# A linear-attention block with a gate: mean and scale of eleven row tiles spread through DRAM, and the order of the steps around it

## The chip, the cores and the metric

The kernel runs on one core of one Trainium2 chip. The metric is the device time of one execution in microseconds.

## The reference

For x of 2048 rows and 576 columns (one batch), with 32 heads of 18 columns:

```python
xn = layernorm(x)                       # (x - m) / sqrt(v + 1e-5)
q, k, v = split(xn @ wqkv)              # 32 heads of 18
phi = lambda t: where(t > 0, t + 1, exp(t)) + 1e-6
pq, pk = phi(q), phi(k)
kv  = einsum("bhsd,bhse->bhde", pk, v)  # one 18 x 18 state per head
z   = einsum("bhsd->bhd", pk)
o   = einsum("bhqd,bhde->bhqe", pq, kv) / (einsum("bhqd,bhd->bhq", pq, z) + 1e-6)
s   = o @ wo
g   = silu((gelu(x @ w_gate) * (x @ w_up)) @ w_down)   # 4608 inner columns
out = x + s * g
```

The change concerns the layer normalization and the order in which k, v, the state `kv` and some of the q products are made.

## The kernel before

**Rows and words.** The 2048 rows are 16 tiles of 128, four tiles to a block (`TT` = 4), and two blocks to each half `s`; `N0` = 8 is the first tile of the second half. The 576 columns are two halves of 288, each laid out as 128 + 128 + 32, the 32 columns three times over. A float32 operand of a long product is cut into two words: a high word, copied by ScalarE (ACT) to the type fp32r, and a low word, the difference, taken by VectorE (DVE). `to_operand` (L281) makes both words of a tile of x: one ACT copy of 384 columns and two DVE subtractions for each of its halves. A product of two such operands takes seven passes for a half, so a part of a tile is 14 matmuls. The weights of k and v are cut into three parts of 416, 412 and 388 columns (`TW`), so a tile has 42 matmuls.

**Normalization.** Tiles 0 to 3 are normalized by rows and then turned by TensorE (PE). Tiles 4 to 15 are loaded twice, two tiles at a time (`load_x`): by rows for the moments, and already turned. `spread` (L169) takes mean and variance with bn_stats and starts the scale with ACT's logarithm and exponential; `scales` (L185) refines the scale on DVE by one step of Newton; `x_next(n)` is both of them for tiles n and n+1. That leaves a mean and a scale on each row's partition, while the turned tile has the rows along its columns and needs both values on all partitions. For this `turn` (L208) lets PE turn the mean and the scale of each row, each taken 128 times over, into a PSUM tile `ms`:

```python
pin(nc.tensor.transpose(t[:, i * P : (i + 1) * P], v.to_broadcast([P, P]), ident))  # L214
```

`normalize` (L228) then is one DVE subtraction of 768 columns and two DVE products of 384, with `ms` as second operand, and `to_operand` behind it. `place(n)` calls it for tiles 4 to 15, `save` does nothing for these.

**A tile of k and v.** `kv_tile(t)` (L492) writes out this order, and `pin` keeps it on every engine: part 0 of the tile's products (`x_mm`); on even t the products of the pair t-2, t-1 that add to the state (`kv_pair`, `kv_mm`; 20 short matmuls for each tile, into the PSUM tile `kv_a`, column groups 0 to 3 of 126 and group 4 of 72); `turn(t+1)`; `k_post(t, 0)`, which evacuates k's columns of part 0 (DVE, `e_k` and `pk`); part 1; `place(t+1)`; `k_post(t, 1)`, at whose end ACT takes the exponential of `e_k` and GpSimd (POOL) adds it to `pk`; `v_post(t, 1)`, ACT's copies of v to `va`; part 2; the steps in `end`, with the moments of later tiles among them; and `v_post(t, 2)`. A tile t with t mod 8 = 7 does not prepare its follower.

**Buffers.** The products of k, v and q, and `ms`, share six PSUM banks; `kv_a` has its own. `pk`, `va` and three pieces of a sum share four SBUF slots. `gl_tile` hands out six SBUF slots that the q tiles use too.

**Between tiles 7 and 8, and behind tile 15.** Four q products for each of two blocks come between tiles 7 and 8 (`q_store`: 14 matmuls, an evacuation in `phi` with ACT, DVE and a POOL add, and a store to DRAM), and for the other two behind tile 15 (`q_hold`, kept in SBUF). The dictionaries `behind` and `ahead` place other steps behind each: moments, sums of x for the fast products of the gate (`difference`; `form` and `form_apart` make words of a sum and store them), the masked state (`kv_done`) and its product with wo (`kv_wo`). The fifth group of a q block (`gi` = 4) is only four transposes. `prep_q`, in tiles 4 to 7, cuts the weights of q, with the subtractions on POOL.

**Queues.** Loads and stores are issued by SyncE (SP) in program order. `load_x(n+4)` stands behind tiles 4, 6, 8 and 10, `form("T4")` with its store at the end of tile 9.

Of the kernel before, what the change touches and what calls it, by code (L numbers as in the profile page):

```python
# [8 lines left out]
F32 = mybir.dt.float32  # L9
# [82 lines left out]
def block_kernel(ctx, tc, x, xe, xt, wq_d, wkv_d, wo, wgu_d, wd_d, out):  # L92
# [92 lines left out]
    def scales(n0):  # L185

        n, mv, st = mom.pop(n0)
        v, r, c = (st[:, i, 0:n] for i in range(1, 4))
        if n == 1:
            vec("tensor_scalar", c, r, r, -0.5, op0=ALU.mult, op1=ALU.mult)  # L190
            vec("tensor_scalar", c, c, v, 1.5, op0=ALU.mult, op1=ALU.add)
            vec("tensor_scalar", c, c, r, None, op0=ALU.mult)
        else:
            vec("scalar_tensor_tensor", c, r, -0.5, r, op0=ALU.mult, op1=ALU.mult)
            vec("tensor_mul", c, c, v)
            vec("scalar_tensor_tensor", c, c, 1.5, r, op0=ALU.add, op1=ALU.mult)
        for t in range(n):
            scale_of[n0 + t] = mv[:, t, 0:1], c[:, t : t + 1]

    def center(n):  # L200

# [6 lines left out]
    def turn(n, new=bank):  # L208

        xs = xstat[n // 2][:, n % 2]  # L210
        if n >= TT:
            xts[n] = t = bank(f"ms_{n}")
            for i, v in enumerate(scale_of.pop(n)):
                pin(nc.tensor.transpose(  # L214
                    t[:, i * P : (i + 1) * P], v.to_broadcast([P, P]), ident
                ))
            return
        tiles = [new(f"xt_{n}_{j}") for j in range(2)]
        xts[n] = [t[:, 0 : 3 * P].rearrange("p (k t) -> p k t", k=3) for t in tiles]
        for j in range(2):  # L220
            for k in range(3):
                pin(nc.tensor.transpose(xts[n][j][:, k, :], xs[:, j, k * P : (k + 1) * P], ident))
# [4 lines left out]

    def normalize(n, s, b, c):  # L228

        ms = xts.pop(n)  # L230
        xs = xstat[n // 2][:, n % 2, D:].rearrange("p (k t) -> p k t", k=6)
        m, r = (ms[:, None, i * P : (i + 1) * P] for i in range(2))
        vec("tensor_sub", xs, xs, m.to_broadcast([P, 6, P]))
        for j, nm in enumerate(BS[b]):
            if nm not in xo[s]:
                xo[s][nm] = big(2 * b + j, [P, 5, TBN], F32R, f"xo_{s}_{nm}")
                new_plain(s, nm)
            vec(
                "tensor_mul", xf[s][nm][:, :, c], xs[:, 3 * j : 3 * j + 3],
                r.to_broadcast([P, 3, P]),  # L240
            )
        for nm in BS[b]:
            to_operand(xo[s][nm], xf[s][nm], c)
# [32 lines left out]
        if last:  # L276
            xts.pop(n)

    mom, scale_of, xts = {}, {}, {}

    def to_operand(o, src, c):  # L281
        act(o[:, 0:3, c], src[:, :, c], AF.Copy)
# [110 lines left out]
        act(e, e, AF.Exp, scale=-1.0)  # L393
        pool("tensor_add", o, o, e)

    def kv_mm(t):
        if t == 0:
            acc.append(own_bank("kv_a"))
        pk, va = pks.pop(t), vas.pop(t)
        for gi, wdt in enumerate(WIDTHS):  # L400
            for half in range(2):
                o, cs = kv_out(gi, half)
                mm(
                    o, va[:, 2 * gi + half, 0 : o.shape[0]],
                    pk[:, gi * GW + cs.start : gi * GW + cs.stop],
                    start=(t == 0 and gi == 0), stop=(t == S // P - 1),
                    skip_group_check=True,
                )
# [8 lines left out]
    def x_mm(t, c, js=(0, 1), passes=KV_PASSES):  # L417

        tb, i = divmod(t, TT)
        s, b = divmod(tb, 2)  # L420
        begin = (t, c) not in pkv
        if begin:
            pkv[t, c] = bank(f"kv_{t}_{c}")
        o = pkv[t, c]
        for j in js:
            for n, (wi, xi) in enumerate(passes):
                mm(
                    o[:, 0 : TW[c]], xo[s][BS[b][j]][:, xi, i * P : (i + 1) * P], kv_part(c, j, wi),
                    start=(begin and j == 0 and n == 0), stop=(j == 1 and (wi, xi) == (2, 2)),
                )  # L430
# [61 lines left out]
    def kv_tile(t, mid_=(), end=()):  # L492

        ahead = t % (2 * TT) != 2 * TT - 1
        x_mm(t, 0)
        if t % 2 == 0:
            kv_pair(t)
        if ahead:
            turn(t + 1)
        k_post(t, 0)  # L500
        x_mm(t, 1)
        if ahead:
            place(t + 1)
            save(t + 1)
        run(list(mid_))
        k_post(t, 1)
        v_post(t, 1)
        x_mm(t, 2)
        run(list(end))
        v_post(t, 2)  # L510

    def kv_pair(t):

        for i in (t - 2, t - 1):
            if i in vas:
                kv_mm(i)

    ph, ph_d = {}, {}

# [904 lines left out]
    def x_next(n):  # L1424

        if n % 2 == 0:
            spread(n, 2)
            scales(n)
        center(n)
# [17 lines left out]
    load_q(0)  # L1447
    for n in range(3, 2 * TT):
        ends = []
        if n < 2 * TT - 2:  # L1450
            ends.append(lambda n=n: x_next(n + 2))
        if n >= TT:
            j, c = divmod(n - TT, 2)
            prep_q(c, j)
            if n == TT + 1:
                load_q(1)
        if n == 2 * TT - 1:
            ends += [lambda i=i: difference(0, i) for i in range(3)]
        kv_tile(n, end=ends)
        if n in (4, 6):  # L1460
            load_x(n + 4, 2)
        if n == TT:
            for nm in BS[0]:
                keep(0, nm, xo[0][nm])
        if n == TT:
            q_store(0, 4)
        if n == TT + 3:
            keep(0, "B22", xo[0]["B22"])
# [3 lines left out]
    def form(nm):  # L1472
        keep(0, nm, build(0, nm, 12))

    def form_apart(nm):
# [11 lines left out]
        dma(out=d[:, 2], in_=last[:, 0].bitcast(F32))  # L1487

    behind = {
        (0, 0): [lambda: kv_pair(N0), lambda: spread(N0, 2), lambda: difference(0, 3)],  # L1490
        (0, 1): [
            lambda: scales(N0), lambda: form("T1"), lambda: q_store(1, 4),
        ],
        (0, 2): [lambda: form_apart("T3")],
        (0, 3): [lambda: turn(N0)],
        (1, 0): [lambda: place(N0)],
        (1, 1): [lambda: form("T2"), lambda: spread(N0 + 2, 2), lambda: scales(N0 + 2)],
    }
# [3 lines left out]
            run(behind.get((tb, gi), []))  # L1502
    for n in range(N0, 2 * N0):
        ends = []
        if n < 2 * N0 - 2:
            ends.append(lambda n=n: center(n + 2) if n == N0 else x_next(n + 2))
        if n == N0 + 1:
            ends.append(lambda: form("T4"))
        if n == 2 * N0 - 3:
            ends.append(load_wo)  # L1510
        if n == 2 * N0 - 2:
            ends.append(make_sel)
        if n == 2 * N0 - 1:
            ends += [lambda i=i: difference(1, i) for i in range(3)]
        kv_tile(n, end=ends)
        if n in (N0, N0 + 2):
            load_x(n + 4, 2)
    ahead = {
        (2, 0): [lambda: kv_pair(2 * N0), kv_done, spread_sel, lambda: difference(1, 3)],
        (2, 1): [lambda: kv_wo(4), lambda: q_hold(2, 7, 4)],  # L1520
        (2, 2): [lambda: kv_wo(0), lambda: kv_wo(1), move_rows],
        (2, 3): [lambda: kv_wo(2), lambda: kv_wo(3)],
        (3, 0): [lambda: den(2), lambda: q_hold(3, 8, 4)],
# [117 lines left out]
```

## Time and profile before

| | |
|---|---|
| median of three runs | 1456.73 us (1456.26 to 1457.28) |
| profiled execution | 1456.62 us |
| its span in the trace | 1454.9 us |
| granted TensorE clock | 1.0 |
| busy: PE, weight loads | 1447.7 us (100%), 1290.2 us (89%) |
| busy: DVE, ACT, POOL | 1152.8 us (79%), 562.5 us (39%), 579.1 us (40%) |
| DMA | 233.98 MB, 161 GB/s in the mean |

Times of instructions are us in one profiled execution; a line number L126 is that of the helper that records every DVE operation (L123 is ACT's, L129 PE's matmuls, L132 POOL's), so a group is told by its tiles, written out<-in. PEld is the loading of PE's weights, which overlaps its matmuls, and SPq the queue of DMA issues. In the chain of waits a line gives the start in us, the step's length, engine, tile, line and the count of instructions. In the view by groups, three figures after a count are the shortest, the median and the longest in ns, followed by when the first and the last began. A releaser row ("PEld ms <- DVE st") gives the summed idle time, the number of waits and the longest, in us.

### The profile page before, as it was taken

To read this page: it belongs to the slowest core of one execution; us is meant where nothing else is said; L and a number is where in the kernel's file an instruction comes from. 1 tells how busy PE (TensorE), PEld (TensorE's weight loads), DVE (VectorE), ACT (ScalarE), POOL (GpSimd) and SP (SyncE) were. 2 spreads that over 40 slices of the span, in tenths; PEclk is the share of its full clock that TensorE was granted. 3 is DMA by queue.
4 is the path that set the end of the run, shared out by engine and by line. 5 is a ranking of instruction groups with operands and counts; after the bars stand their busy time and mean duration, and the time that the engine had idled before them with its cause. 6 is when DMAs were issued, how large, how long until landed. Compare 5 with 4: busy or idle time off the path is not lost.

```text
span 1454.9 us, 22180 instructions
## 1 busy us (share of the span) xinstructions
PE 1447.7 (100%) x8286; PEld 1290.2 (89%) x8286; DVE 1152.8 (79%) x1605; ACT 562.5 (39%) x914; POOL 579.1 (40%) x520
## 2 busy tenths in 40 slices
PE   9999999999999999999999999999999999999998
PEld 8989989988888888888888888888889999999998
DVE  7687767376787887887778878787888978989898
ACT  6443355332222233322322232332235555545454
POOL 3342340225756567565575765667632000000000
PEclk9999999999999999999999999999999999999999
DMA  5543115521432315224242243324389888767886
GB/s 222 191 191 140 38 31 211 211 107 51 161 102 107 130 51 186 90 94 138 77 155 87 100 147 108 110 88 132 115 282 343 263 263 254 246 189 233 278 288 222
DMA packets 118085, 233.98 MB, mean 161 GB/s; under 512 B 11018, under 2 KB 44682, under 8 KB 116058
## 3 DMA queue, kind: packets, MB, share of 16 engines
q1 hardware_dynamic: 115178, 220.31, 44.8%
q0 software_dynamic: 2656, 12.06, 2.2%
q8 instruction: 65, 1.06, 0.3%
q14 instruction: 42, 0.34, 0.1%
q10 hardware_dynamic: 144, 0.20, 0.0%
HBM read 149.91 MB, written 82.58 MB: 160 GB/s over the span
## 4 chain that ended last, share of the span: by engine, by line
PE 94%; DVE 3%; DMA 2%; issue 0%; ACT 0%; SPq 0%; POOL 0%; DVEq 0%; ACTq 0%; POOLq 0%
PE bd L129 21%; PE al L859 16%; PE de L859 16%; PE ga L859 16%; PE kv L129 8%; PE be L859 8%; PE s L129 4%; PE q L129 4%; DMA raw_h<-hs 1%; DVE sx L126 1%; PE kv_a L129 1%; DMA sx<-in_x_dram 0%; DVE raw_h L126 0%; DVE acc L126 0%; PE idle L129 0%
## 5 line engine op out<-in xcount | busy, mean ns | idle before, releaser
L132 POOL TENSOR_TENSOR sm<-raw 128x384 f32<-128x384 f32 x72 | 75.5, 1048 | 146.7 <-DMA raw<-in_wgu_dram 104.8
L129 PE MATMUL kv<-wkv,xo_B 128*128 128x412 f32 (+2 forms) x662 | 125.5, 348 | 0.0
L126 DVE TENSOR_TENSOR wa<-sm,wa 128x768 fp32r<-128x768 f32 x72 | 95.1, 1321 | 36.1 <-ACT wa L123 35.3
L129 PEld LDWEIGHTS kv<-wkv,xo_B 128*128 128x128 f32 x662 | 119.9, 188 | 1.0 <-ACT xo_B L123 0.2
L129 PE MATMUL bd<-w_head,hi 128*128 128x288 f32 x516 | 117.9, 294 | 0.0
L126 DVE TENSOR_TENSOR wa<-raw,wa 128x256 fp32r<-128x256 f32 x72 | 67.7, 940 | 51.5 <-ACT wa L123 48.3
L126 DVE TENSOR_TENSOR wb<-raw,wb 128x256 fp32r<-128x256 f32 (+1 forms) x108 | 101.9, 944 | 7.3 <-ACT wb L123 5.8
L123 ACT ACTIVATE hi<-raw_h 128x1024 fp32r<-128x1024 f32 x59 | 62.6, 1061 | 95.5 <-PE bd L129 65.3
L129 PE MATMUL bd<-w_end,hi 128*128 128x288 f32 x448 | 89.8, 294 | 0.0
L123 ACT ACTIVATE spot_h<-spot_h 128x512 f32<-128x512 f32 x49 | 30.8, 635 | 150.1 <-DVE spot_h L126 150.1
L126 DVE TENSOR_TENSOR raw_h<-raw_h,hi 128x1024 fp32r<-128x1024 f32 x59 | 71.8, 1223 | 20.3 <-ACT hi L123 20.2
L129 PEld LDWEIGHTS bd<-w_head,hi 128*128 128x128 f32 x516 | 87.0, 188 | 0.1
L129 PE MATMUL bd<-w_end,raw_h 128*128 128x288 f32 x264 | 77.9, 295 | 0.0
L123 ACT ACTIVATE wa<-sm 128x1152 fp32r<-128x1152 f32 x36 | 41.8, 1162 | 87.8 <-PE de L859 87.8
L123 ACT ACTIVATE u<-al 128x512 f32<-128x512 f32 x72 | 41.0, 594 | 89.5 <-PE al L859 81.2
L129 PEld LDWEIGHTS bd<-w_end,hi 128*128 128x128 f32 x448 | 71.9, 188 | 0.0
L129 PE MATMUL bd<-beside,raw_h 128*128 128x288 f32 x240 | 70.8, 295 | 0.0
L132 POOL TENSOR_TENSOR spot_h<-spot_h,spot_h 128x512 f32<-128x512 f32 x45 | 62.5, 1396 | 2.9 <-DVE spot_h L126 2.4
L859 PE MATMUL al<-xo_B,wa 128*128 128x512 f32 x252 | 63.0, 389 | 0.0
L859 PE MATMUL al<-xr_B,wa 128*128 128x512 f32 x252 | 63.0, 389 | 0.0
L859 PE MATMUL be<-xo_T,wa 128*128 128x512 f32 x252 | 63.0, 389 | 0.0
L859 PE MATMUL be<-xr_T,wa 128*128 128x512 f32 x252 | 63.0, 389 | 0.0
(274 smaller groups left out, 4040.6 us busy)
## 6 DMA issues: line engine op xcount, KB each, us to landing
raw_h<-hs SPq DMA_DIRECT2D x176, 256.0 KB
raw<-in_wgu_dram SPq DMA_DIRECT2D x36, 768.0 KB
hs<-spot_h SPq DMA_DIRECT2D x90, 256.0 KB
hs<-spot_g SPq DMA_DIRECT2D x80, 256.0 KB
b<-in_wd_dram SPq DMA_DIRECT2D x42, 432.0 KB
hs<-spot_m SPq DMA_DIRECT2D x38, 256.0 KB
raw_g<-hs SPq DMA_DIRECT2D x22, 256.0 KB
raw_a<-hs SPq DMA_DIRECT2D x20, 256.0 KB
```

The costliest lines, as they stand in the source:

```text
L123: pin(nc.scalar.activation(*args, **kw))
L126: pin(getattr(nc.vector, op)(*args, **kw))
L129: pin(nc.tensor.matmul(*args, **kw))
L132: pin(getattr(nc.gpsimd, op)(*args, **kw))
L859: nc.tensor.matmul(o, w[0:rows, wi, :], xop[0:rows, xi, :], start=(start and n == 0), stop=(n == len(PASSES) - 1), skip_group_check=True,)
```

## The change

`scales` for tiles 4 and on copies the two means beside the two scales, writes these 128 x 4 values to DRAM (`md`), and reads them back into all partitions (`mr`, 128 x 4 values on each, in a `gl_tile` slot). `normalize` takes mean and scale of tiles 5 to 15 from there, with steps of four values; `turn` remains for tile 4 alone. In `kv_tile`, for tiles from 5 on that prepare a follower, `place(t+1)` goes ahead of `k_post(t, 0)`. `kv_pair` does groups 0 to 3 of both tiles and then group 4 of both. The moments of tiles 6 and 7 move from the end of tile 4 to that of tile 3, those of 12 and 13 from tile 10 to 9, those of 14 and 15 from tile 12 to 11; `form("T4")` moves from the end of tile 9 to that of 10. Two transposed q groups move one place forward, `q_store(1, 4)` behind the first q product and `q_hold(2, 7, 4)` behind the first of block 2; `turn(8)` goes.

```diff
--- before.py
+++ after.py
@@ -196,6 +196,17 @@
             vec("scalar_tensor_tensor", c, c, 1.5, r, op0=ALU.add, op1=ALU.mult)
         for t in range(n):
             scale_of[n0 + t] = mv[:, t, 0:1], c[:, t : t + 1]
+        if n0 >= TT:
+            vec("tensor_copy", st[:, 3, 2:4], mv[:, 0:2, 0])
+            d = dr.tile([P, 4], F32, name=f"md_{n0}")
+            g = gl_tile([P, P, 4], f"mr_{n0}")
+            dma(out=d, in_=st[:, 3, :])
+            dma(
+                out=g.rearrange("p t c -> p (t c)"),
+                in_=d.rearrange("t c -> (t c)")[None, :].to_broadcast([P, 4 * P]),
+            )
+            for t in range(n):
+                rows_of[n0 + t] = [g[:, None, :, i + t] for i in (2, 0)]
 
     def center(n):
 
@@ -208,7 +219,9 @@
     def turn(n, new=bank):
 
         xs = xstat[n // 2][:, n % 2]
-        if n >= TT:
+        if n > TT:
+            return
+        if n == TT:
             xts[n] = t = bank(f"ms_{n}")
             for i, v in enumerate(scale_of.pop(n)):
                 pin(nc.tensor.transpose(
@@ -227,9 +240,12 @@
 
     def normalize(n, s, b, c):
 
-        ms = xts.pop(n)
+        if n in xts:
+            ms = xts.pop(n)
+            m, r = (ms[:, None, i * P : (i + 1) * P] for i in range(2))
+        else:
+            m, r = rows_of.pop(n)
         xs = xstat[n // 2][:, n % 2, D:].rearrange("p (k t) -> p k t", k=6)
-        m, r = (ms[:, None, i * P : (i + 1) * P] for i in range(2))
         vec("tensor_sub", xs, xs, m.to_broadcast([P, 6, P]))
         for j, nm in enumerate(BS[b]):
             if nm not in xo[s]:
@@ -276,7 +292,7 @@
         if last:
             xts.pop(n)
 
-    mom, scale_of, xts = {}, {}, {}
+    mom, scale_of, xts, rows_of = {}, {}, {}, {}
 
     def to_operand(o, src, c):
         act(o[:, 0:3, c], src[:, :, c], AF.Copy)
@@ -393,11 +409,11 @@
         act(e, e, AF.Exp, scale=-1.0)
         pool("tensor_add", o, o, e)
 
-    def kv_mm(t):
-        if t == 0:
+    def kv_mm(t, groups):
+        if not acc:
             acc.append(own_bank("kv_a"))
-        pk, va = pks.pop(t), vas.pop(t)
-        for gi, wdt in enumerate(WIDTHS):
+        pk, va = pks[t], vas[t]
+        for gi in groups:
             for half in range(2):
                 o, cs = kv_out(gi, half)
                 mm(
@@ -492,14 +508,17 @@
     def kv_tile(t, mid_=(), end=()):
 
         ahead = t % (2 * TT) != 2 * TT - 1
+        early = ahead and t > TT
         x_mm(t, 0)
         if t % 2 == 0:
             kv_pair(t)
-        if ahead:
+        if early:
+            place(t + 1)
+        elif ahead:
             turn(t + 1)
         k_post(t, 0)
         x_mm(t, 1)
-        if ahead:
+        if ahead and not early:
             place(t + 1)
             save(t + 1)
         run(list(mid_))
@@ -511,9 +530,12 @@
 
     def kv_pair(t):
 
-        for i in (t - 2, t - 1):
-            if i in vas:
-                kv_mm(i)
+        pair = [i for i in (t - 2, t - 1) if i in vas]
+        for groups in (range(4), (4,)):
+            for i in pair:
+                kv_mm(i, groups)
+        for i in pair:
+            del pks[i], vas[i]
 
     ph, ph_d = {}, {}
 
@@ -1447,8 +1469,8 @@
     load_q(0)
     for n in range(3, 2 * TT):
         ends = []
-        if n < 2 * TT - 2:
-            ends.append(lambda n=n: x_next(n + 2))
+        if n == TT - 1:
+            ends.append(lambda: x_next(TT + 2))
         if n >= TT:
             j, c = divmod(n - TT, 2)
             prep_q(c, j)
@@ -1487,12 +1509,12 @@
         dma(out=d[:, 2], in_=last[:, 0].bitcast(F32))
 
     behind = {
-        (0, 0): [lambda: kv_pair(N0), lambda: spread(N0, 2), lambda: difference(0, 3)],
-        (0, 1): [
-            lambda: scales(N0), lambda: form("T1"), lambda: q_store(1, 4),
+        (0, 0): [
+            lambda: kv_pair(N0), lambda: q_store(1, 4), lambda: spread(N0, 2),
+            lambda: difference(0, 3),
         ],
+        (0, 1): [lambda: scales(N0), lambda: form("T1")],
         (0, 2): [lambda: form_apart("T3")],
-        (0, 3): [lambda: turn(N0)],
         (1, 0): [lambda: place(N0)],
         (1, 1): [lambda: form("T2"), lambda: spread(N0 + 2, 2), lambda: scales(N0 + 2)],
     }
@@ -1502,9 +1524,9 @@
             run(behind.get((tb, gi), []))
     for n in range(N0, 2 * N0):
         ends = []
-        if n < 2 * N0 - 2:
-            ends.append(lambda n=n: center(n + 2) if n == N0 else x_next(n + 2))
-        if n == N0 + 1:
+        if n in (N0 + 1, N0 + 3):
+            ends.append(lambda n=n: x_next(n + 3))
+        if n == N0 + 2:
             ends.append(lambda: form("T4"))
         if n == 2 * N0 - 3:
             ends.append(load_wo)
@@ -1516,8 +1538,11 @@
         if n in (N0, N0 + 2):
             load_x(n + 4, 2)
     ahead = {
-        (2, 0): [lambda: kv_pair(2 * N0), kv_done, spread_sel, lambda: difference(1, 3)],
-        (2, 1): [lambda: kv_wo(4), lambda: q_hold(2, 7, 4)],
+        (2, 0): [
+            lambda: kv_pair(2 * N0), kv_done, lambda: q_hold(2, 7, 4), spread_sel,
+            lambda: difference(1, 3),
+        ],
+        (2, 1): [lambda: kv_wo(4)],
         (2, 2): [lambda: kv_wo(0), lambda: kv_wo(1), move_rows],
         (2, 3): [lambda: kv_wo(2), lambda: kv_wo(3)],
         (3, 0): [lambda: den(2), lambda: q_hold(3, 8, 4)],
```

## The prediction

> **What bounds the kernel now.** I read the page first, then the chain of waits over the first 150 us, then DVE, POOL and ACT in order of time beside it.
>
> ```profile
> PE 1447.7 (100%) x8286; PEld 1290.2 (89%) x8286; DVE 1152.8 (79%) x1605; ACT 562.5 (39%) x914; POOL 579.1 (40%) x520
> ```
>
> PE is busy all the time, so a microsecond counts only where PE gains or loses it. The change touches the first 180 us: the tiles of k and v (42 products each) and the q products between tiles 7 and 8. From the chain there:
>
> ```profile
> 48.23 0.36 PE ms L214 x2
> 56.72 0.22 PE ms L214 x2
> 64.64 1.31 PE kv_a L129 x40
> 117.56 7.75 PE kv L129 x42
> ```
>
> A pair of turns costs PE 0.22 us between long products and 0.36 behind the products of a pair of tiles (`kv_a`, 1.31 us); a tile is 7.75 us, about 2.6 for each of its three parts. PE waits once in this stretch, for the second turn of tile 12, whose scale comes late from DVE (first row below). DVE sets the rest, and in two places it is full:
>
> ```profile
> PEld ms L214 <- DVE st L126: 1.1, 1, 1.1
> 56.50:62.90 6.40, 6.40 (x38) 6.33 (x37) 6.01 (x12) 2.64 (x5) 3.43 (x4) 1.00 1.02 430
> 84.00:98.00 14.00, 14.00 (x66) 11.49 (x65) 13.31 (x21) 8.71 (x15) 6.36 (x5) 1.00 0.43 174
> 144.00:175.00 31.00, 31.00 (x231) 30.48 (x228) 20.46 (x48) 9.11 (x25) 11.34 (x20) 1.00 0.14 44
> DVE e_k L126 <- PE kv L129: 1.0, 1, 1.0
> ```
>
> The middle rows are stretches of time; after the length come PE, PEld and DVE: DVE is busy for 6.01 of 6.40, 13.31 of 14.00, but 20.46 of 31.00 us. The last row is the longest of DVE's waits from 83 to 123 us. So DVE has slack in tiles 12 to 15 and hardly any in tile 5 and from the q products to tile 10.
>
> **What goes.** Eleven pairs of turns, tiles 5 to 15: 11 x 0.22 = 2.4 us (3.1 if the five behind short products give all of their 0.36). Tile 12's wait: 1.1. One change between long and short products fewer at each of eight pairs: the nearest rows are the two kinds of turns, 0.14 apart for two of them, so at most 8 x 0.14 = 1.1, perhaps nothing; such a change is smaller than a new kind of product, and I take 0.2. Together 3.7. The profiled execution took 1456.62 us (span 1454.9 us), 0.1 under the median of the three times, 1456.73, so I use it as it is: without a new wait it becomes 1452.9.
>
> **What the normalization becomes.** A tile has one subtraction of 768 columns and two products of 384:
>
> ```profile
> L126 DVE TENSOR_TENSOR x<-x,ms x12: 943/953/955, 40.0 to 162.6; 128x768 f32<-128x768 f32 x12
> L126 DVE TENSOR_TENSOR xf_B<-x,ms x24: 545/551/555, 41.0 to 164.1; 128x384 f32<-128x384 f32 x24
> ```
>
> Their second operand lay in PSUM (`ms`); now it lies in SBUF, like the first. What that means beside POOL:
>
> ```profile
> 58.13 0.95 DVE L126 TENSOR_TENSOR x<-x,ms 128x768 f32<-128x768 f32 x1
> 57.36 1.29 POOL L132 TENSOR_TENSOR ph<-ph,e_q 128x512 f32<-128x512 f32 x1 [2.40 <-DVE ph L126]
> 58.61 0.75 POOL L132 TENSOR_TENSOR wq<-rq,wq 128x256 fp32r<-128x256 f32 x1
> 60.13 0.73 POOL L132 TENSOR_TENSOR wq<-rq,wq 32x256 fp32r<-32x256 f32 x1
> 60.25 1.98 DVE L126 TENSOR_TENSOR xo_B<-xf_B,xo_B 128x256 fp32r<-128x256 f32 x4
> 50.76 1.50 DVE L126 TENSOR_TENSOR xo_B<-xf_B,xo_B 128x256 fp32r<-128x256 f32 x4
> 77.26 6.46 DVE L126 TENSOR_TENSOR xf_B<-xf_B,xf_B 128x1536 f32<-128x1536 f32 x3
> 77.85 2.46 POOL L132 TENSOR_TENSOR pk<-pk,e_k 128x576 f32<-128x576 f32 x1 [1.75 <-ACT e_k L123]
> 86.33 1.75 DVE L126 TENSOR_TENSOR xf_B<-xf_B,xf_B 128x1536 f32<-128x1536 f32 x1
> 63.44 1.43 POOL L132 TENSOR_TENSOR pk<-pk,e_k 128x576 f32<-128x576 f32 x1 [2.57 <-ACT e_k L123]
> ```
>
> The subtraction against PSUM at 58.13 takes its usual 0.95 although POOL works through all of it. Four subtractions out of SBUF at 60.25 take 1.98 instead of 1.50; at 77.26 both sides lose: three operations of 1.75 take 6.46, and POOL's add 2.46 instead of 1.43. The two do not run together; the later one stands until the other is through. So a DVE operation on two SBUF operands that meets a POOL add loses 1.0 to 1.2 us (6.46 - 5.25), one that meets a weight subtraction 0.47, and POOL may lose as much. The normalization was free of this; now it will meet POOL in most tiles, because it stands right behind the evacuations, when POOL adds pk.
>
> Two more things follow from the order. The tile's own e_k and pk come 3.7 us later in DVE's queue, and the exponential, POOL's add and the pair products hang on them. And the moments of tiles 12 and 14 are taken at the end of odd tiles, whose last copies of v on ACT queue behind the logarithm; the pair that needs them starts a third of a tile later.
>
> **The four places where this reaches PE.** First, the pair of tiles 4 and 5:
>
> ```profile
> 56.52 0.69 DVE L126 TENSOR_SCALAR ph<-q 128x512 f32<-128x512 f32 x1 [0.49 <-ACT e_q L123]
> 62.26 0.32 DVE L126 TENSOR_SCALAR e_k<-kv 128x160 f32<-128x160 f32 x1
> ```
>
> PE reaches tile 5's half of it at 64.64 + 0.65 = 65.3, now 0.6 earlier (two turns): 64.7. Tile 6's normalization (58.13 to 62.26, 4.13 with one weight subtraction met) now meets the q add (1.0) and two more weight subtractions (0.9): e_k comes 1.9 later, less 0.6 that the earlier PE may give back. POOL's add of pk starts at 63.44 + 1.3 to 1.9, meets tile 7's normalization, which is now ahead (0.3), takes 1.43 and a small memset 0.1: 66.6 to 67.2. PE waits 1.9 to 2.5; I take 2.0. The moments of tiles 6 and 7, moved from tile 4 to tile 3, help DVE here; that it waits for ACT and PE in between keeps most of this from counting.
>
> Second, the start of tile 9:
>
> ```profile
> 111.19 0.58 DVE L126 TENSOR_SCALAR e_k<-kv 128x416 f32<-128x416 f32 x1
> 112.18 0.94 DVE L126 TENSOR_TENSOR x<-x,ms 128x768 f32<-128x768 f32 x1
> 115.85 0.32 DVE L126 TENSOR_SCALAR e_k<-kv 128x160 f32<-128x160 f32 x1
> 113.75 0.99 ACT L123 ACTIVATE xo_B<-xf_B 128x384 fp32r<-128x384 f32 x2 [2.53 <-DVE xf_B L126]
> 109.64 7.70 PE kv L129 x42
> 108.94 0.16 DVE L126 SCALAR_TENSOR_TENSOR st<-st 128x2 f32<-128x2 f32 x1 [0.40 <-ACT st L123]
> ```
>
> PE comes at 109.64 + 5.1 = 114.7, when ACT's copies end (113.75 + 0.99): no slack. Tiles 8 and 9 each meet a q add (2 x 1.1, and about 0.3 each for which the first operation stands), and two small copies of the means (0.15 each, by the small operation at 108.94) come on top: 3.1. Tile 9's normalization is ahead of e_k and pk, which gives back 1.0 (111.19 to 112.18), and the earlier turns 0.4. PE waits 1.7.
>
> Third, the pair of tiles 8 and 9, and fourth, of 10 and 11:
>
> ```profile
> 79.08 3.20 PE q L129 x14
> 131.78 0.33 DVE L126 TENSOR_SCALAR e_k<-kv 128x160 f32<-128x160 f32 x1
> 134.82 0.49 ACT L123 ACTIVATE va<-kv 128x252 f32<-128x252 f32 x2
> 125.03 1.92 DVE L126 TENSOR_TENSOR xo_T<-xf_B,xo_T 128x1024 fp32r<-128x1024 f32 x2 [2.23 <-ACT xo_T L123]
> 127.01 0.34 SPq L135 DMA_DIRECT2D kept_T<-xo_T  x1
> 130.13 0.37 SPq L135 DMA_DIRECT2D x<-in_x_dram  x1
> GB/s 399 365 86 0 35 203 279 410 400 102 0 238 231 45 232 412 402 182 0 0 0 0 0 0 0 298 447 438 123 241 392 416 103 0 0 0 0 0 0 0
> ```
>
> With the moments behind it, a tile's last e_k is followed by its last v copy 3.5 us later (131.78 to 135.3). From tile 9's start PE has 7.75 + 2.6 + 0.65 = 11.0 to tile 9's half of the pair. DVE has 1.5 left of tile 9, 1.5 of evacuations, tile 10's normalization 3.7 with the pk add of tile 8 in it (1.1), 1.0 of evacuations and those 3.5: 12.3. PE waits 1.3 to 1.4. From there to tile 11's half of the next pair PE has 0.65 + 5.2 + 7.75 + 3.25 = 16.8; DVE 0.4, 3.7, 1.5, T4's split with its wait 4.1 (row 125.03, moved here from tile 9), 3.7, 1.5 and 3.3: 18.2, so 1.4. On top, SP now issues the load of tile 14 behind T4's store. The last row is what DMA moved in slices of 1.1 us from 100 us: store and load each take some 4 us in it, so the x rows land about 6.5 after the store's issue, and DVE wants them 5.2 after it: 1.3 more, hidden if the two transfers overlap. I take 3.1 with the spread in lengths, from 1.4.
>
> Sum: 2.0 + 1.7 + 1.4 + 3.1 = 8.2 of new waits against 3.7 gained: 4.5 slower, **1461.1 us**.
>
> The trip through DRAM itself I cost at nothing: two DMAs in sequence six times, on SP ahead of later loads and stores. By the nearest rows, which are far larger transfers of about 4 us, a trip ends at most 8 us after the moments, less for 2 and 256 KB; between moments and use lie 7 us or more. At the far end DVE would stand 1 us in three tiles. The two q steps moved forward bring the same instructions earlier; kv_done's products still have a whole q product (3.20 us, row at 79.08) before they are used. Tiles 12 to 15 meet POOL too (4 x 1.1), in DVE's 10.5 us of slack.
>
> **Rivals.** *Half rate.* The spread operand steps over four values per column, and the rows show no stepped operand. If DVE reads it at half rate, the 1.05 ns per column ((953 - 551) / 384) doubles for these operations: 0.8 + 2 x 0.4 = 1.6 us a tile. Tiles 5 to 12 lie where DVE has no slack: 8 x 1.6 = 12.8, and the time is 1473.9. Against it: nothing measured; DVE's rows are at about one rate whatever the operands. Chance 0.25.
>
> The Trainium skill, page "SBUF — State Buffer", Specifications (TRN2), speaks for that rival: SBUF has lines of 16 bytes, and an access pattern needs at least two hits in a line for full bandwidth. Four floats are 16 bytes, so each column would be a new line; the page gives no price for VectorE, and no run here shows one yet.
>
> *Faster.* The early start of the normalization outweighs the meetings: DVE is never later than PE at the four places, and all 3.7 us stay: 1452.9. It decides at slack: DVE would have to be on time by 2.0 us at the pair of tiles 4 and 5 and by 3.1 at that of 10 and 11. For it speaks that a normalization needs nothing from PE any more; against it the 13.31 of 14.00. Chance 0.13.
>
> *Only the queue behind the logarithm.* The meetings fall into gaps, but tile 11's v copies are late by 1.4 to 3.1: 1452.9 + 2.3 = 1455.2, no change. The same follows if the turns' time does not leave PE because it waits for the tile instead. Chance 0.16.
>
> **How the numbers follow.** Forecast 0.46, half rate 0.25, queue only 0.16, faster 0.13. The forecast's own range is 1458.0 (the fourth wait at 1.4, the first three a little shorter) to 1466.0 (a meeting more in each of tiles 5, 8, 9 and 10). A measurement of this kernel can tell about 0.2% (2.9 us) from no change: under 1453.8 is faster, over 1459.6 slower. Slower takes the forecast and the half rate, 0.71; same 0.16; faster 0.13. The range leaves out the faster rival and the outer ends: 1455.0 to 1474.0.
>
> **What would show it.** Right: `x` and `xf_B` operations with `mr` of about 0.95 and 0.55 us alone, but 1.5 to 2.2 where a POOL add or weight subtraction runs, with POOL's adds stretched too; no `ms` after tile 4; PE waiting for `va`, `pk` or `xo_B` at the four places, 8 us in all before 150 us. Half rate: `x` at 1.75 also where POOL is idle. Wrong: normalizations at 0.95 beside POOL, or PE without waits there.

## The result, and the profile after

The changed kernel took 1469.56 us (median of four, 1468.47 to 1472.41) against 1456.9 for the kernel before: 1.0089 times as long, 95% interval 1.0077 to 1.0102, or 12.7 us more. The profiled execution took 1468.47 us with a span of 1466.8, 11.9 over the span before.

PE's time, in order of time, at the four places that the prediction names (start, length, and in brackets how long PE stood idle before and for whom):

```profile
65.52 0.72 PE L129 MATMUL kv_a<-pk,va 128*64 128x72 f32 x16
69.07 0.86 PE L129 MATMUL kv_a<-pk,va 128*64 128x72 f32 x24 [2.83 <-POOL va L132]
...
121.39 5.78 PE L129 MATMUL kv<-wkv,xo_B 128*128 128x416 f32 x21 [3.40 <-ACT xo_B L123]
...
134.84 0.61 PE L129 MATMUL kv_a<-pk,va 128*64 128x72 f32 x16 [0.28 <-ACT va L123]
...
153.77 0.47 PE L129 MATMUL kv_a<-pk,va 128*64 128x72 f32 x8 [1.72 <-POOL va L132]
155.30 0.61 PE L129 MATMUL kv_a<-pk,va 128*64 128x72 f32 x16 [1.06 <-ACT va L123]
```

The pairs of tiles 4 and 5, 8 and 9, 10 and 11, and the start of tile 9: all four places have a wait: 2.83, 0.28, 2.78 (1.72 + 1.06) and 3.40 us. Before the pair at 65.52, tile 6's first part also stretches by 1.4 us while its words arrive. Behind tile 13 nothing differs any more: from there on every product starts some 12 us later than before.

The normalization, by its tiles (shortest, median and longest in ns, then first and last start):

```profile
L126 DVE TENSOR_TENSOR x<-x,mr x11: 1525/1548/2154, 48.6 to 169.2; 128x768 f32<-128x768 f32 x11
L126 DVE TENSOR_TENSOR xf_B<-x,mr x22: 835/867/1990, 50.2 to 172.6; 128x384 f32<-128x384 f32 x22
```

Tile 4, still served by PE, has the old durations (943 and 550 ns); the eleven others take 1.53 us at least where it was 0.95, and 0.84 at least where it was 0.55. Even the shortest is slow, so this is no matter of what runs beside it. On top of that come the long ones, and POOL's side of them, between the q products and tile 9 (DVE, then POOL, in order of time):

```profile
102.17 2.15 DVE L126 TENSOR_TENSOR x<-x,mr 128x768 f32<-128x768 f32 x1
104.36 2.60 DVE L126 TENSOR_TENSOR xf_B<-x,mr 128x384 f32<-128x384 f32 x2
101.65 3.84 POOL L132 TENSOR_TENSOR ph<-ph,e_q 128x512 f32<-128x512 f32 x2 [1.44 <-DVE ph L126]
```

The two q adds of the last row take 3.8 us together, where an add beside no such operation takes 1.29; at 116.29 two more take 3.80. Both sides lose time when they meet.

By stretches of time (length; then PE, PEld, DVE, ACT, POOL busy; granted clock, DMA share, GB/s) there is one thing more, a clock below 1 behind the waits. In the trace's records it is 1.00 or 0.50, and it changes only at points that lie whole multiples of 3.41 us apart, a grid. So the stretches here are those between grid points:

```profile
64.30:67.72 3.42, 1.94 (x23) 1.50 (x21) 3.33 (x6) 1.51 (x5) 0.99 (x1) 1.00 0.96 324
67.72:71.13 3.41, 2.06 (x31) 2.02 (x32) 3.09 (x3) 1.64 (x3) 2.01 (x4) 1.00 0.22 87
71.13:74.54 3.41, 3.41 (x21) 3.41 (x19) 3.29 (x7) 0.03 (x1) 1.64 (x3) 1.00 0.86 291
118.92:122.33 3.41, 0.94 (x5) 0.93 (x6) 3.31 (x6) 1.05 (x2) 1.17 (x1) 1.00 0.74 231
122.34:125.74 3.40, 3.40 (x12) 3.27 (x11) 3.31 (x7) 1.34 (x5) 0.58 (x1) 0.50 0.90 291
153.05:156.46 3.41, 1.63 (x27) 1.44 (x28) 2.84 (x11) 1.05 (x5) 0.67 (x2) 1.00 0.18 74
156.47:159.87 3.40, 3.40 (x12) 3.26 (x11) 3.29 (x6) 1.05 (x2) 0.00 (x0) 0.50 0.18 42
```

DVE is busy for 3.1 to 3.3 of 3.4 us around the first two waits. Behind the wait at tile 9, and behind the waits at the pair of 10 and 11, PE runs at half its clock for one stretch: 12 products where the full stretch at 71.13 has 21. Behind the wait of 2.83 it does not. That wait lies across a grid point: PE stands idle for 1.48 us of the stretch before the point and 1.35 of the one behind it, against 2.47 and 1.78 in the two stretches that are followed by half the clock.

### The profile page after: what moved, and what is told of

Read it like the earlier page. It is cut to its first block, busy times and chain, and to the rows that moved or that the text cites. A ratio compares the mean times of both kernels' runs of the same rounds, so it can differ in the third digit from the quotient of the medians.

```text
span 1466.8 us, 22154 instructions
## 1 busy us (share of the span) xinstructions
PE 1450.3 (99%) x8264; PEld 1291.6 (88%) x8264; DVE 1166.3 (80%) x1611; ACT 562.2 (38%) x914; POOL 589.8 (40%) x520
## 3 DMA queue, kind: packets, MB, share of 16 engines
q8 instruction: 65, 1.06, 0.3%
## 4 chain that ended last, share of the span: by engine, by line
PE 93%; DVE 5%; ACT 1%; issue 1%; DMA 0%; POOL 0%; SPq 0%; DVEq 0%; POOLq 0%; ACTq 0%
PE bd L129 25%; PE al L881 16%; PE de L881 16%; PE ga L881 16%; PE be L881 8%; PE kv L129 5%; PE s L129 4%; PE q L129 2%; DVE xf_B L126 1%; DVE x L126 1%; PE kv_a L129 1%; DVE xo_B L126 0%; DVE xo_T L126 0%; DMA x<-in_x_dram 0%; DVE bn L126 0%
## 5 line engine op out<-in xcount | busy, mean ns | idle before, releaser
L129 PE MATMUL kv<-wkv,xo_B 128*128 128x412 f32 (+2 forms) x662 | 128.9, 354 | 4.1 <-ACT xo_B L123 3.4
L129 PEld LDWEIGHTS kv<-wkv,xo_B 128*128 128x128 f32 x662 | 123.0, 192 | 7.0 <-ACT xo_B L123 4.5
L881 PE MATMUL de<-xo_T,wa 128*128 128x512 f32 x252 | 63.0, 389 | 0.0
L881 PE MATMUL ga<-xo_T,wa 128*128 128x512 f32 x252 | 63.0, 389 | 0.0
L881 PE MATMUL de<-xr_T,wa 128*128 128x512 f32 x252 | 63.0, 389 | 0.0
```

Of the source, the lines that this page charges most:

```text
L129: pin(nc.tensor.matmul(*args, **kw))
L881: nc.tensor.matmul(o, w[0:rows, wi, :], xop[0:rows, xi, :], start=(start and n == 0), stop=(n == len(PASSES) - 1), skip_group_check=True,)
```

## The experiments

Three theories stood: the step of 16 bytes in the spread operand makes DVE slow (A, with the meetings of DVE and POOL on top); a second operand from SBUF is slow by itself (B); the order of the queues does it (C). The theories' letters are those of the expectations. Every ratio is against the kernel before on the same chip; the runs used several chips, on which the kernel before took 1456.7 to 1456.9 us. The diffs show the main lines only.

**Mean and scale as rows in DRAM**, so that the step is one value:

```diff
-            d = dr.tile([P, 4], F32, name=f"md_{n0}")
-            g = gl_tile([P, P, 4], f"mr_{n0}")
+            d = dr.tile([4, P], F32, name=f"md_{n0}")
+            g = gl_tile([P, 4, P], f"mr_{n0}")
-            dma(out=d, in_=st[:, 3, :])
+            dma(out=d.rearrange("c t -> t c"), in_=st[:, 3, :])
...
```

> The changed kernel, but mean and scale lie in four rows of 128 in DRAM and in the spread tile, so DVE reads them in steps of one value, not four. Theory A (the step of 16 bytes costs rate, and the meetings of DVE and POOL come on top): the subtraction alone falls from 1.54 to about 0.95 us and a product from 0.85 to 0.55, in meetings with POOL they stay up to 1.1 longer; of the 12.0 us some 7 go and about 5 stay, 1461 us. Theory B (any second operand from SBUF is slower than one from PSUM, whatever its step): durations and time stay, 1469 us. Theory C (the time goes by the order of the queues alone): durations fall, the time by less than 2 us.

Measured: 1491.37 us, 1.0238 (1.0223 to 1.0253). The time misses all three. The durations and DVE's waits tell why:

```profile
L126 DVE TENSOR_TENSOR x<-x,mr x11: 950/959/1199, 54.1 to 195.6; 128x768 f32<-128x768 f32 x11
L126 DVE TENSOR_TENSOR xf_B<-x,mr x22: 545/556/1650, 55.0 to 198.1; 128x384 f32<-128x384 f32 x22
DVE x L126 <- DMA mr<-md: 34.2, 6, 8.9
```

The medians are those of PSUM, so theory B falls: an operand out of SBUF without the step costs nothing by itself. But the write to DRAM now goes in 512 pieces of 4 bytes. From its issue to that of the read that waits for it took 8.9 us or more, where 128 pieces of 16 bytes take 1.4 when nothing else moves. DVE waits 34.2 us for it. The run's time says nothing of the step's cost; its durations say that the rate follows the step.

**The same with steps of two values**, without the small pieces:

```diff
-            d = dr.tile([P, 4], F32, name=f"md_{n0}")
-            g = gl_tile([P, P, 4], f"mr_{n0}")
+            d = dr.tile([2, P, 2], F32, name=f"md_{n0}")
+            g = gl_tile([P, 2, P, 2], f"mr_{n0}")
...
```

> The changed kernel, but mean and scale of one tile lie beside each other, and the two tiles one behind the other: DVE reads them with steps of two values (8 bytes) in place of four, with no copy by ACT. By the rule of the Trainium skill (page 'SBUF — State Buffer', Specifications: two hits in a line of 16 bytes give full bandwidth) the subtraction alone takes 0.95 us and a product 0.55. Theory of step and meetings: durations alone as just said, beside POOL up to 1 us longer as in the run with SBUF and no step; four waits of PE stay at about half; 1461 to 1464 us. If meetings alone had made the waits, the time stays at 1468 to 1470 us. If the step alone, 1457 to 1459 us, with the wait at the pair of tiles 10 and 11 only. If rate goes by the step itself and not by the line, the subtraction alone lies between 0.95 and 1.54.

Measured: 1462.97 us, 1.0041 (1.0027 to 1.0055).

```profile
L126 DVE TENSOR_TENSOR x<-x,mr x11: 948/959/2067, 48.9 to 165.2; 128x768 f32<-128x768 f32 x11
L126 DVE TENSOR_TENSOR xf_B<-x,mr x22: 544/558/1675, 49.9 to 167.8; 128x384 f32<-128x384 f32 x22
66.90 0.97 PE L129 MATMUL kv_a<-pk,va 128*64 128x72 f32 x24 [1.75 <-POOL va L132]
119.16 7.11 PE L129 MATMUL kv<-wkv,xo_B 128*128 128x416 f32 x37 [1.87 <-ACT xo_B L123]
131.51 0.47 PE L129 MATMUL kv_a<-pk,va 128*64 128x72 f32 x8 [1.06 <-POOL va L132]
132.29 0.61 PE L129 MATMUL kv_a<-pk,va 128*64 128x72 f32 x16 [0.30 <-ACT va L123]
151.88 0.61 PE L129 MATMUL kv_a<-pk,va 128*64 128x72 f32 x16 [2.07 <-ACT va L123]
```

With 8 bytes the full rate is back, and 6.6 us of the 12.7 go (1469.56 to 1462.97), although this layout's trip is slower (DVE waits 4.1 us for it in all). The step of 16 bytes alone cost about half. The lines are from the slowest of this kernel's four executions, 1465.21 us. The Trainium skill, page "SBUF — State Buffer", Specifications (TRN2), has the rule: at least two hits in a line of 16 bytes. Two values per line run at 959 and 558 ns, one value per line at 1548 and 867, so the trace agrees; the price on VectorE, which the page does not give, is a factor of 1.6 here (1.7 for each further column: 681 against 401 ns for 384), not two. And the rest of the picture is the prediction's likeliest case: waits at the four places, with no step: 1.75, 1.87, 1.36 (1.06 + 0.30) and 2.07 us.

**ACT copies mean and scale to a PSUM bank, and to SBUF.** Two kernels that differ only in where the copy goes:

```diff
+    def to_bank(n):
+        g, i = rows_of.pop(n)
+        xts[n] = t = bank(f"ms_{n}")                      # to PSUM
+        xts[n] = t = xstat[n // 2][:, n % 2, 0 : 2 * P]   # in the other kernel: to SBUF
+        act(t[:, 0 : 2 * P].rearrange("p (c t) -> p c t", c=2),
+            g.rearrange("p t (c i) -> p i c t", c=2)[:, i], AF.Copy)
...
+        if ahead and t >= TT:
+            to_bank(t + 1)
         x_mm(t, 0)
```

> The changed kernel, but ACT copies mean and scale of each tile from the spread tile to a PSUM bank one tile ahead (256 columns, about 0.5 us of ACT for each of 11 tiles), and DVE reads them from there, as before the change; the order is that of the changed kernel. Theory A with meetings: subtraction 0.95 and products 0.55 also beside POOL, POOL's add of pk at 1.43; the waits of PE at the pair of tiles 4 and 5 and at the start of tile 9 go, a wait of 2 to 3 us stays at the pair of tiles 10 and 11 because of the moved moments and store; 1455 to 1457 us. Theory C (the order, whatever the rate): the four waits stay at half their size or more, over 1462 us.

> The changed kernel, but ACT copies mean and scale of each tile one tile ahead, as in the run with PSUM, to contiguous columns in SBUF (the tile's plain rows, which are not needed any more). DVE reads a second operand from SBUF without the step. Theory A with meetings: alone 0.95 and 0.55, beside POOL up to 1.1 longer, and POOL's adds longer too; waits at the pairs and at the start of tile 9 between those of the changed kernel and those of the run with PSUM: about 5 us of the 12, 1461 to 1464 us. If the step alone had cost the time, the same as with PSUM, 1462.4 us with no wait but the one at the pair of tiles 10 and 11; if any SBUF operand is slow, 1.54 and 0.85 again and 1469 us.

Measured: to PSUM 1462.42 us, 1.0038 (1.0023 to 1.0053); to SBUF 1468.46, 1.0074 (1.0058 to 1.0089). First PSUM, then SBUF:

```profile
L126 DVE TENSOR_TENSOR x<-x,ms x12: 944/955/957, 40.1 to 164.5; 128x768 f32<-128x768 f32 x12
L126 DVE TENSOR_TENSOR xf_B<-x,ms x24: 547/552/555, 41.1 to 165.9; 128x384 f32<-128x384 f32 x24
```

```profile
L126 DVE TENSOR_TENSOR x<-x x11: 957/959/1856, 48.8 to 171.7; 128x768 f32<-128x768 f32 x11
L126 DVE TENSOR_TENSOR xf_B<-x x22: 546/558/1531, 49.8 to 173.2; 128x384 f32<-128x384 f32 x22
```

The medians are almost equal, the longest are not: out of PSUM no operation exceeds 957 ns, whatever POOL does; out of SBUF one reaches 1856. Nothing else of the program differs, so the 6.0 us between the two are the meetings' price in this order, with the clock behind the longer waits in it. The Trainium skill, same page, section "Who interferes with whom", says that an instruction of VectorE with two inputs in SBUF contends with a GpSimd instruction that reads SBUF; the trace agrees, and shows that one input in PSUM is free of it. Both kernels came out 4.5 us and more over what theory A gave for them (1455 to 1457, and 1461 to 1464). Two things that were not counted are in the traces: ACT's copies stand in ACT's queue behind other work (DVE waits 16 us for them in each), and the clock falls to 0.50 for 3.4 us, once in the kernel with PSUM, behind the wait that was expected to stay at the pair of tiles 10 and 11, and twice in the other. How the excess divides between them was not measured.

**The normalization where it was before**, with everything else changed:

```diff
-        early = ahead and t > TT
+        early = False
```

> The changed kernel, but with each tile's normalization behind the evacuation of the tile's first part, where it was before the change; the spread, its step of four values and the moved moments stay. Theory A (the longer operations cause the waits): the operations stay at 1.54 and 0.85 alone, the time changes by 2 us or less, 1466 to 1470 us. Theory C (the order causes the waits): the waits at the pairs go, 1460 us or less.

Measured: 1467.11 us, 1.0066 (1.0049 to 1.0083). As theory A said (1466 to 1470). Theory C asked for 1460 or less: as a cause of the whole loss the early place falls, since without it PE still waits 5.4 us for `xo_B`. It may cost 2.4 us here (1469.56 against 1467.11), but the two intervals overlap. The other moves in the order are still in this kernel.

**PE's turns kept, with the new order**:

```diff
-        if early:
-            place(t + 1)
-        elif ahead:
+        if ahead:
             turn(t + 1)
+        if early:
+            place(t + 1)
```

(the block in `scales` that goes to DRAM is left out, and `turn` does all tiles again).

> The changed kernel, but PE turns mean and scale of every tile as before; nothing goes through DRAM. The order (normalization ahead, short products of a pair last, moved moments, store and q groups) is that of the changed kernel. Theory A: the normalization is as fast as before, so only the wait at the pair of tiles 10 and 11 is left (2 to 3.6 us), and the turns' 2.4 us are back: 1458 to 1460 us. Theory C: the waits stay, 1465 us or more.

Measured: 1460.64 us, 1.0025 (1.0015 to 1.0034), just over theory A's 1460. Without the spread one place remains where PE waits long, the pair of tiles 10 and 11, and its chain is plain. The chain of waits of the changed kernel shows the same one:

```profile
145.50 0.32 SPq L135
145.82 0.05 issue
145.87 6.54 DMA x<-in_x_dram
152.43 0.83 DVE bn L126 x2
...
154.45 0.30 ACT st L123
154.78 0.20 ACT st L123
154.98 0.28 ACT va L123
155.26 0.04 issue
155.30 0.61 PE kv_a L129 x16
```

SP issues T4's store, then the load of tiles 14 and 15; the load takes 6.5 us; DVE takes the moments; ACT the logarithm; and only behind that come tile 11's last copies of v, for which PE waits.

**The load ahead of the store, then also the copies of v ahead of the moments**, both on the kernel with turns:

```diff
+        if n == N0 + 2:
+            ends.append(lambda: load_x(N0 + 6, 2))
             ends.append(lambda: form("T4"))
...
+        if t in (2 * TT + 1, 2 * TT + 3):   # the second kernel only
+            v_post(t, 2)
+            run(list(end))
+            return
```

> The kernel with the turns kept and the new order, with one thing more: the load of the x rows of tiles 14 and 15 is issued ahead of T4's store, not behind it. If the wait at the pair of tiles 10 and 11 comes from SP's queue (the load issued at 136.8 behind the store, landing at 143.5, the logarithm behind it and tile 11's copies of v behind the logarithm), the rows land some 3 us earlier, the wait of 2 to 3 us falls to 1.6 or less, and the slow clock behind it goes too: 1456 to 1457.5 us. If the wait is DVE's own lateness, it stays: 1460.6 us.

> The kernel with the turns kept, the new order and the load of tiles 14 and 15 ahead of T4's store, and with one thing more: in tiles 9 and 11 the last copies of v go ahead of the moments. The wait left at the pair of tiles 10 and 11 (1.1 us, for the copies behind the logarithm) goes: 1456 to 1456.8 us, 0.3 to 1 us under the kernel before. If the wait was DVE's, 1457.7 us again.

Measured: 1457.69 us, 1.0005 (0.9996 to 1.0014), and 1456.37 us, 0.9998 (0.9989 to 1.0007). The first lies 0.2 over the range of the queue's theory, the second within its range. The gain of the first mend is clear of noise, that of the second is not: the two intervals overlap. In three views of PE's waits (sum, times, longest), with turns, with the load ahead, with both (in the last no wait for ACT is left; 0.4 to 0.5 us for POOL are in all three):

```profile
PE kv_a L129 <- ACT va L123: 2.1, 1, 2.1
```

```profile
PE kv_a L129 <- ACT va L123: 0.3, 1, 0.3
```

```profile
PE kv_a L129 <- POOL va L132: 0.4, 1, 0.4
```

4.3 us hung on this queue, of which 2.1 are the wait itself; with it goes half the clock for 6.8 us behind it (1.00 in the other two). Its other executions fit that: of the nine of the kernel with turns, eight had a mean clock of 0.998 or 0.999 and spans of 1458.3 to 1460.1 us, and one had 1.000 and 1456.2.

**Matmuls that nobody reads in the place of two waits**:

```diff
+        if t == 2 * TT + 1:
+            fill(t, 0, 17)      # 17 products of 416 columns into the bank of the next part
         x_mm(t, 0)
+        if t == 3 * TT:
+            fill(t, 1, 15)
```

> The changed kernel, with matmuls that nobody reads while PE would wait: 17 of 416 columns (3.2 us) ahead of tile 9's first part, where PE waits 3.6 us, and 15 of 412 columns (2.8 us) ahead of the pair of tiles 10 and 11, where it waits 3.2 us. If the slow matmuls behind these two waits (granted clock 0.73 and 0.66 in the 5 us) come from the waits, the clock stays at 1.0 and about 2.5 to 3 us go: 1466 to 1467 us. If they come from data that arrive late, the time stays at 1469 us or rises by up to 1 us.

Measured: 1469.72 us, 1.0091 (1.0077 to 1.0104): as long as without, and 2.7 over what was expected if the waits were the cause. By its time alone the run would speak for data that arrive late. The stretches behind the two filled places (first two rows), and two others:

```profile
120.00:125.00 5.00, 4.74 (x26) 4.36 (x25) 4.84 (x8) 1.05 (x2) 1.97 (x1) 1.00 0.56 174
155.00:160.00 5.00, 5.00 (x61) 4.68 (x60) 4.40 (x13) 1.05 (x5) 0.68 (x2) 1.00 0.20 66
69.18:72.58 3.40, 3.04 (x29) 2.91 (x30) 2.54 (x4) 1.67 (x3) 1.52 (x4) 0.50 0.24 26
137.45:140.85 3.40, 3.40 (x11) 3.27 (x11) 3.33 (x5) 1.05 (x2) 0.00 (x0) 0.50 0.06 10
```

Where PE was kept busy the clock stayed at 1.00, so those slow stretches come from the waits. But the clock now fell behind two other waits, so this trace has two stretches at half the clock, as many as that of the changed kernel. One of these waits, 2.81 us at the pair of tiles 4 and 5, is the wait that the changed kernel had passed at 1.00. Here 2.44 us of it lie between two grid points; there it was cut into 1.48 and 1.35.

All fourteen traces, each cut at its own grid between 12 and 210 us, say the same. Fourteen stretches at full clock have PE idle for 1.89 us or more of the 3.41, and behind every one of them the clock is 0.50. Behind none with 1.61 or less does it fall. In between, at 1.66 to 1.79, it falls behind five of seven. Those five hold the short products of a pair, the other two do not; that this decides is not shown. The grid lies elsewhere in each trace (the first change of the clock is at 4.4 to 7.7 us), so whether a wait of this size costs clock is partly chance. The Trainium skill, page "TensorE: Matmul & The Clock Gate", Part 1, tells of a free-running window of about 3.4 us; the stretches of 3.41 us in these traces agree.

**The change mended, three ways.** The PSUM kernel with both mends of the queue; that with ACT's copies earlier; and the kernel with steps of two values with both mends.

```diff
-            (1, 0): [lambda: place(N0)],
+            (1, 0): [lambda: place(N0), lambda: to_bank(N0 + 1)],   # second kernel
...
         x_mm(t, 2)
+        if ahead and t + 2 > TT and (t + 2) % (2 * TT) != 0:        # second kernel
+            to_bank(t + 2)
```

(In tiles 10 and 12 the steps in `end` go ahead of that copy.)

> The kernel with mean and scale copied to PSUM by ACT, with two things more: the load of tiles 14 and 15 ahead of T4's store, and in tiles 9 and 11 the last copies of v ahead of the moments. If step, meetings and this queue are all that the change lost by, PE waits less than 1 us between tile 5 and tile 15 and the gain of the turns is left: 1453.5 to 1455.5 us. If the spread has a cost that is not found yet (ACT's copies, SP's issues), 1457 us or more.

> The kernel with mean and scale in PSUM and both mends of the queue, with one thing more: ACT makes its copies earlier (tile 9's behind tile 8's normalization, between the q products; the others ahead of the last copies of v of the tile before), so that DVE does not wait for them (0.5 us ahead of tile 9's and 1.9 ahead of tile 10's before). The waits of PE at the start of tile 9 (1.2) and at the pair of tiles 8 and 9 (1.1 to 1.6) go, and what is left is the turns' gain and the second turn's wait of tile 12: 1453.5 to 1455 us. If the copies only move the lateness into ACT's queue, 1456 us or more.

> The changed kernel with steps of two values in place of four and both mends of the queue (the load of tiles 14 and 15 ahead of T4's store; in tiles 9 and 11 the last copies of v ahead of the moments). What is left against the run with PSUM, both mends and early copies (1456.4 us) is that the second operand lies in SBUF, so DVE and POOL meet, and that DVE waits for the trip where the write of 8 bytes a value pair is slower (4.1 us of waits in the run before, 0.8 to 2.3 at a time). Theory of meetings: waits of PE stay at the pair of tiles 4 and 5 (1.8), at the start of tile 9 (1.9) and at the pair of tiles 8 and 9 (1 to 2), and none at the pair of tiles 10 and 11: 1459.5 to 1462 us. If the queue had been all that was left, 1457 us or less.

Measured: 1459.51 us, 1.0014 (1.0005 to 1.0023), 4 us over its expectation and where a cost not found yet was expected (1457 or more); 1456.40 us, 0.9997 (0.9988 to 1.0006), over it too, by 1.4, where lateness in ACT's queue was expected (1456 or more; DVE still waits 5.3 us for them, against 15.8 in the first kernel with PSUM); 1460.26 us, 1.0024 (1.0015 to 1.0034), as the theory of meetings said. PE's waits of the second and of the third:

```profile
PE kv_a L129 <- POOL va L132: 1.2, 2, 0.6
PE kv L129 <- ACT xo_B L123: 0.4, 1, 0.4
```

```profile
PE kv L129 <- ACT xo_B L123: 1.9, 1, 1.9
PE kv_a L129 <- POOL va L132: 1.6, 1, 1.6
```

With the operand in PSUM and the queue mended the spread equals the turns (1456.40 and 1456.37); it does not beat them. In the last kernel what is left is meetings, the clock behind one wait and the slower trip (DVE waits 3.8 us for it), together 3.9 us more.

So the 12.7 us divide, by steps between kernels: 6.6 the step of 16 bytes (1469.56 to 1462.97), 2.7 the queue with the clock behind it (to 1460.26) and 3.9 the operand in SBUF with its trip (to 1456.40). That is 13.2; the mended change lies 0.5 under the kernel before (1456.9), which is not told from nothing. The parts depend on the order in which they are taken away: with turns the queue was worth 4.3.

## Why the prediction was right and wrong

**The time**: slower, as forecast, but by 12.7 us and not 4.5. The forecast of 1461.1 and its own range, 1458.0 to 1466.0, missed. The stated range, 1455.0 to 1474.0, holds 1469.56 because it was drawn to take in the half-rate rival, which had a chance of 0.25.

**The bound**: right. All that happened lies between 47 and 175 us, and it is PE's waits and PE's clock.

**What goes**: the turns are gone from tile 5 on, and the wait for tile 12's scale too. Against the kernel before, PE's delays in the changed kernel add to about 15.4 us (waits and slow stretches, by the starts of its products) while the span grew by 11.9, so 3.5 came back, near the forecast's 3.7. The change between long and short products, for which I took 0.2 in all, is 0.02 for a pair.

**The normalization**: the step that failed is the one that left the durations at 0.95 and 0.55 in the likeliest case. The half-rate rival had the mechanism, and the sign named for it, a long `x` also where POOL is idle, is there, at 1.53 us and not 1.75. Its price was too high: 0.59 and 0.31 us, 1.2 a tile, not 1.6. With the measured price its own sum is 1461.1 + 8 x 1.2 = 1470.7, beside 1469.56. That it comes so close is partly luck: the step cost 6.6 us and not 9.6, and the kernel without it took 1463.0 and not 1461.1. I held against it that DVE's rows had one rate whatever the operands, but no row had such an operand: that was no evidence.

**The meetings**: right. Operations out of SBUF stretch beside POOL and those out of PSUM do not (957 against 1856 ns at the longest), and POOL loses as well.

**The four places**: right in place. In size they are best compared with the kernel without the step, since that is what the sum was for, though its trip is slower: 2.0, 1.7, 1.4 and 3.1 forecast, 1.75, 1.87, 1.36 and 2.07 measured, 8.2 against 7.1. With the step the first two grew to 2.83 and 3.40, and the third shrank to 0.28, probably since PE was late already.

**What the sum lacked**: the clock. In the profile before, PE has no wait over 1.1 us and the clock is 1.00 throughout, so I priced a wait at its own length. In the changed kernel two stretches of 3.41 us at half the clock cost about 2.6 us beside the waits. The kernel without the step has two such stretches too, behind its first wait and behind its last, which fits that it took 1463.0 and not 1461.1, although its waits were shorter than forecast.

**The trip through DRAM**: at nothing, right in the changed kernel, where DVE waits for it nowhere. With pieces of 8 and 4 bytes DVE waited 4.1 and 34.2 us.

**The other rivals**: the faster one fell at the slack that it needed. The queue-only rival was a real part, the fourth place, but not alone.

## What to carry to other kernels

A value that moves from PSUM to SBUF changes three things for the engine that reads it: the step at which it is read (16 bytes was slow here, 8 and 4 were not), the meetings with POOL, and whose queue brings it there. Look at each, and lay the values close together. A wait of the engine that is the bound can cost more than its length, because the clock may fall behind it: here half the clock for 3.4 us whenever PE had stood idle for 1.89 us or more of a stretch of 3.41 before. A move that frees that engine gains nothing while another engine sets the pace a microsecond later. Where a step is moved ahead of others on a queue, follow what is then behind it: here a load behind a store, a logarithm behind the load and a copy behind the logarithm cost 2.7 to 4.3 us, more than the 2.4 of the eleven turns.

## What was not expected of the hardware

- From the issue of a write of 2 KB to DRAM to the issue of the read that waits for it took 1.4 us in 128 pieces of 16 bytes when nothing else moved, 3.1 to 4.6 in 256 pieces of 8, and 8.9 to 11.8 in 512 of 4.
- The step of 16 bytes slows DVE's operation by a factor of 1.6 (1548 against 959 ns), a step of 8 bytes not at all.
- Almost the same wait at the same place can cost clock or not. At the start of tile 9 PE waits 1.87 us in the kernel with steps of two values and 1.92 in the one with both mends of the queue. The first lies across a grid point, with 1.40 us before it, and the clock stays:

```profile
115.28:118.69 3.41, 2.01 (x12) 1.68 (x10) 3.38 (x4) 0.64 (x2) 2.86 (x2) 1.00 0.00 0
118.70:122.10 3.40, 2.94 (x16) 2.92 (x17) 3.15 (x9) 0.88 (x3) 0.00 (x0) 1.00 0.54 185
```

The second lies between two grid points, and the clock falls:

```profile
115.28:118.69 3.41, 1.49 (x8) 1.18 (x7) 3.18 (x6) 0.99 (x2) 1.20 (x1) 1.00 0.23 47
118.70:122.10 3.40, 3.40 (x12) 3.22 (x11) 3.21 (x7) 1.51 (x5) 0.90 (x1) 0.50 0.98 322
```
